# Sketch attention with a squared-ReLU MLP: first weights requested behind the first queries, values padded behind the key sketch copies, and a new planned order

## Chip, cores, metric

One core of one Trainium2 chip. The metric is the device time of one execution in microseconds (us), lower is better. The state of an execution ("fast" or "slow") is known from its time and from the granted TensorE clock in its records; only fast executions are compared unless the text says otherwise. Engines: PE (TensorE, matmuls), DVE (VectorE), ACT (ScalarE), POOL (GpSimd), SP (SyncE, which only issues DMAs here).

## What is computed

```python
# q, k, v: (4 batches, 4 heads, 1088 tokens, 32); S1, S2: (8, 32)
phi(x) = outer(S1 x, S2 x) flattened                 # 64 features per token
kv  = sum over tokens of phi(k) (x) v;  z = sum over tokens of phi(k)
attn = (phi(q) kv) / (phi(q) z + 1e-6)               # a sum over all tokens, not causal
x = attn transposed to (4352 tokens, 128)
out = relu(x @ w_in)**2 @ w_out                      # 128 -> 2048 -> 128
```

The MLP (called "expert" below) is most of the PE work. The attention of the next batch is fed in between its matmuls. Batches are numbered 0 to 3; "the third batch" is batch 2.

## The kernel before

The kernel lists some 620 small operations (`add`), each with the engines that may run it, an assumed duration, and a rank. A planner (`Graph.run`) simulates the engines with these durations and writes out one order; every engine then executes its part of this order strictly in turn. The ranks were found by a search outside of the kernel.

```python
def run(self):                                   # cut: the core of the planner
    ...
    t = max(eng_free.get(e, 0.0), t_slot)
    for d in o.deps: t = max(t, d.end + (SEM if d.eng != e else 0.0))
    ...
    if o.dma is not None:
        first = t + busy - 0.4 + DMA_FIRST       # + 0.4 on POOL
        pipe = max(pipe, first) + o.dma          # 1.85 us for a 544 KB load
        o.end = pipe + DMA_LAST + o.extra
```

Loads that convert or come late are requested by POOL. The first of them stands behind a `gate`, a one-column copy that reads data which must have landed, and each later group is chained: its request first reads one element (`gt`) of the load two groups earlier. The keys of the third and fourth batch also wait for `gate{b}`, a copy that reads the first normalised tokens of the batch before.

```python
o_gate = add("gate", {"POOL": (0.1, 0.15)}, lambda e: nc.gpsimd.tensor_copy(
    gate[96:128], vin[0][96:128, H - 1, 7, D - 1 : D]), [z_ops[0]], -45)   # first values
def cload(name, dst, src, probe, pri, dma, deps=(), new=True):
    ...
    def f(e):
        if mark: nc.gpsimd.tensor_copy(gt[:, 0:1], mark[1])      # waits for an earlier load
        nc.gpsimd.dma_start(out=dst, in_=src)
```

Per batch the attention does, among others (names as in the experiments):

```python
vp{b}.{a}   # ACT or POOL: values copied into a padded tile (a column of ones for z)
tk{b}.{p}   # DVE: keys transposed, kT <- kin, in two parts
ksk, ka, kp # PE sketch of the keys, ACT copy of it, product on DVE or POOL
tq{b}, qr   # DVE: queries transposed, qT <- qin; PE sketch of the queries
mx{b}.{g}   # DVE: den, rec, xs: normalisation of one group of output tokens
tx{b}.{g}, xe{b}.{g}   # PE transposition of xs, copy to xT: from here the expert can run
```

All PE start-up is covered by 30 filler matmuls on zeros (`warm0` to `warm29`, 128x512 each).

Of the kernel before, what the change touches and what calls it, by code (L numbers as in the profile page):

```python
# [19 lines left out]
DGE = 0.43  # L20


RANK = [
    165, 170, 191, 487, 140, 473, 83, 243, 387, 29, 569, 257, 275, 598, 621, 607, 623, 611, 618, 608, 596, 594,
    599, 602, 595, 610, 616, 617, 600, 605, 612, 614, 597, 609, 606, 603, 620, 619, 601, 613, 604, 622, 615,
    121, 85, 496, 286, 292, 31, 53, 582, 435, 476, 79, 120, 298, 526, 415, 475, 574, 355, 338, 160, 178, 10, 14,
    133, 365, 141, 57, 69, 104, 5, 2, 103, 126, 345, 26, 12, 306, 247, 314, 150, 9, 44, 152, 164, 71, 222, 4,
    74, 3, 55, 6, 100, 7, 93, 403, 182, 173, 507, 114, 539, 293, 76, 261, 80, 447, 384, 111, 215, 225, 366, 221,
    276, 299, 394, 17, 78, 92, 39, 145, 1, 135, 203, 193, 15, 98, 64, 52, 313, 382, 389, 357, 130, 369, 401,
    466, 212, 144, 579, 391, 370, 552, 456, 244, 518, 572, 327, 283, 498, 495, 530, 516, 262, 418, 591, 352,  # L30
    368, 564, 543, 485, 348, 477, 575, 316, 465, 302, 437, 542, 310, 188, 479, 201, 440, 49, 263, 147, 129, 199,
    67, 143, 11, 360, 367, 587, 511, 430, 450, 205, 541, 115, 59, 245, 464, 241, 482, 36, 171, 207, 444, 340,
    279, 537, 555, 218, 336, 86, 557, 109, 51, 554, 571, 66, 346, 406, 463, 264, 38, 489, 424, 124, 236, 25,
    250, 439, 371, 46, 350, 200, 392, 514, 154, 118, 8, 198, 18, 297, 206, 290, 524, 474, 462, 565, 592, 404,
    488, 139, 153, 142, 122, 374, 256, 134, 284, 27, 533, 81, 491, 535, 87, 556, 334, 443, 405, 106, 269, 326,
    268, 235, 540, 523, 503, 472, 460, 159, 578, 454, 397, 508, 558, 228, 41, 445, 509, 347, 23, 343, 300, 586,
    224, 291, 469, 471, 213, 28, 285, 20, 88, 50, 589, 77, 242, 33, 240, 132, 68, 398, 237, 204, 500, 90, 321,
    116, 515, 195, 289, 548, 303, 180, 184, 425, 412, 251, 234, 520, 429, 416, 156, 547, 329, 341, 317, 576,
    566, 560, 455, 502, 220, 380, 528, 480, 223, 181, 30, 32, 43, 75, 65, 166, 232, 22, 190, 499, 315, 97, 70,
    501, 72, 434, 127, 570, 417, 119, 158, 174, 373, 157, 253, 332, 484, 230, 214, 101, 532, 301, 238, 162, 216,  # L40
    231, 24, 378, 312, 172, 113, 358, 421, 82, 13, 359, 478, 529, 402, 255, 123, 442, 274, 61, 419, 559, 258,
    361, 45, 567, 536, 265, 525, 550, 545, 308, 395, 505, 583, 531, 325, 385, 590, 427, 335, 457, 110, 295, 519,
    561, 323, 544, 35, 73, 330, 62, 60, 233, 137, 91, 148, 63, 337, 48, 208, 95, 185, 146, 42, 458, 187, 112,
    167, 107, 163, 420, 58, 196, 287, 108, 149, 89, 362, 99, 331, 461, 383, 219, 410, 339, 483, 381, 273, 272,
    517, 259, 254, 436, 451, 534, 551, 319, 549, 584, 270, 356, 21, 453, 280, 490, 414, 553, 376, 521, 294, 396,
    581, 510, 513, 512, 282, 296, 426, 568, 131, 364, 438, 375, 94, 342, 136, 16, 278, 19, 209, 309, 486, 176,
    84, 56, 408, 177, 179, 493, 239, 105, 151, 311, 573, 40, 372, 432, 400, 47, 227, 192, 267, 102, 379, 328,
    585, 407, 377, 304, 506, 422, 563, 271, 189, 305, 527, 96, 428, 459, 186, 117, 217, 522, 37, 54, 388, 288,
    333, 210, 468, 399, 494, 229, 318, 183, 175, 249, 349, 413, 393, 277, 128, 562, 169, 252, 260, 497, 441,
    449, 588, 577, 593, 324, 246, 467, 452, 281, 322, 34, 492, 226, 307, 344, 125, 138, 353, 248, 538, 446, 433,  # L50
    155, 0, 431, 211, 390, 202, 351, 363, 386, 580, 546, 470, 409, 354, 481, 197, 423, 320, 411, 448, 266, 168,
    194, 504, 161,
# [3 lines left out]
    10: 1, 72: 1, 73: 0, 74: 1, 88: 1, 93: 1, 94: 0, 95: 1, 121: 1, 130: 0, 132: 0, 151: 0, 152: 1, 153: 0,  # L56
    174: 1, 178: 0, 187: 1, 188: 1, 202: 1, 207: 0, 208: 0, 209: 1, 210: 1, 234: 0, 242: 1, 244: 0, 258: 1,
    263: 1, 264: 1, 266: 0, 285: 0, 289: 1, 292: 1, 295: 0, 299: 1, 300: 1, 303: 0, 304: 0, 312: 1, 313: 0,
    316: 0, 317: 0, 320: 1, 324: 0, 328: 0, 329: 0, 332: 0, 333: 0, 336: 0, 337: 1, 341: 1, 349: 0, 350: 0,
    353: 0, 357: 0, 358: 0, 361: 0, 362: 1, 365: 0, 369: 0, 370: 0, 373: 1, 374: 0, 378: 1, 390: 0, 391: 1,  # L60
    395: 1, 398: 1, 399: 0, 403: 1, 406: 0, 407: 1, 410: 1, 411: 1, 414: 0, 415: 0, 418: 1, 419: 0, 427: 0,
    436: 1, 439: 0, 440: 0, 443: 0, 444: 0, 447: 0, 448: 0, 452: 0, 456: 1, 468: 0, 469: 0, 473: 1, 476: 0,
    480: 0, 481: 0, 484: 1, 485: 0, 488: 1, 492: 0, 496: 0, 505: 0, 506: 0, 509: 0, 510: 0, 513: 0, 518: 1,
    522: 1, 525: 0, 529: 0, 530: 0, 533: 1, 534: 0, 555: 1, 558: 0, 559: 0, 562: 0, 563: 0, 566: 0, 567: 1,
    571: 0, 574: 1, 584: 0, 587: 0, 592: 0, 595: 1, 604: 0, 608: 0, 609: 0, 613: 0, 616: 0, 617: 1,
# [10 lines left out]
class Op:  # L76
    def __init__(self, name, alts, fn, deps, pri, alloc, uses, port, dma, after, extra):
        self.extra = extra
        self.name, self.alts, self.fn, self.pri = name, alts, fn, pri
        self.deps = [d for d in deps if d is not None]  # L80
        self.alloc, self.uses, self.port, self.dma = alloc, uses, port, dma
        self.after = [d for d in after if d is not None]
        self.look = LOOK
        self.start = self.end = self.eng = None


class Graph:
# [22 lines left out]
    def run(self):  # L110
        eng_free, port_free, pipe, dge = {}, 0.0, 0.0, 0.0
        lanes = []
        todo = {id(o): len(o.deps) + len(o.after) for o in self.ops}
# [6 lines left out]
        while ready:  # L120
            cands = []
            for o in ready:
                t_slot = 0.0
# [12 lines left out]
                for e, (busy, lat, *pen) in o.alts.items():  # L136
                    pen = pen[0] if pen else 0.0
                    t = max(eng_free.get(e, 0.0), t_slot)
# [30 lines left out]
            eng_free[e] = t + busy  # L169
            if e in o.port:  # L170
                port_free = t + busy
# [32 lines left out]
def kernel(  # L204
# [11 lines left out]
    nc = tc.nc  # L216
# [63 lines left out]
    add = G.add  # L280
# [65 lines left out]
    o_gate = add("gate", {"POOL": (0.1, 0.15)}, lambda e: nc.gpsimd.tensor_copy(gate[96:128], vin[0][96:128, H - 1, 7, D - 1 : D]), [z_ops[0]], -45)  # L346
# [3 lines left out]
    def cload(name, dst, src, probe, pri, dma, deps=(), new=True):  # L350
# [10 lines left out]
        o = add(name, {"POOL": (0.85 if mark else 0.6, 3.0)}, f, gated + list(deps) + ([before[0]] if before else []), pri, dma=dma,  # L361
# [50 lines left out]
    def attention(b, vt):  # L412
# [16 lines left out]
        if b == 0:  # L429
            o_kh = [[add(f"ldk{b}.{c0}", SPQ, ld(kin[i], k, c0, c1), (), -230 + c0 / 8, dma=1.85 * (c1 - c0) / 34)] for c0, c1 in ((0, 16), (16, 34))]  # L430
            o_k, o_k2 = o_kh[0][0], o_kh[1][0]
            o_q = [add(f"ldq{b}.{c0}", SPQ, ld(qin[i], q, c0, c1), (), -227 + 2 * c0, dma=2.0 * (c1 - c0) / 34) for c0, c1 in QS]
# [13 lines left out]
            o_gate.deps += o_v[1]  # L446
# [57 lines left out]
        for part, (j0, j1) in enumerate(JP):  # L504
# [25 lines left out]
            prods.append(o_kp)  # L530
# [280 lines left out]
```

## Time and profile before

| | before |
|---|---|
| time, median of 3 runs | 120.3 us (119.84 to 120.82) |
| profiled execution: span, mean granted clock | 118.0 us, 0.995 |
| PE, DVE, ACT busy share | 92%, 82%, 78% |
| third batch's keys (544 KB): request, landing | 39.27, 43.81 (4.5 us later) |
| DVE's first transpose of these keys | starts at 44.07, no idle time ahead of it |

The lines that carry the argument are in the prediction. How to read the last two rows: an engine takes its instructions in the planned order, so a load only costs time when its reader reaches the head of its engine's queue before the load has landed. Here DVE has other work until the keys are in (it is busy with `g` until 44.15).

### The profile page before, as it was taken

To read this page: it belongs to the slowest core of one execution; us is meant where nothing else is said; L and a number is where in the kernel's file an instruction comes from. 1 tells how busy PE (TensorE), PEld (TensorE's weight loads), DVE (VectorE), ACT (ScalarE), POOL (GpSimd) and SP (SyncE) were. 2 spreads that over 40 slices of the span, in tenths; PEclk is the share of its full clock that TensorE was granted. 3 is DMA by queue.
4 is the path that set the end of the run, shared out by engine and by line. 5 is a ranking of instruction groups with operands and counts; after the bars stand their busy time and mean duration, and the time that the engine had idled before them with its cause. 6 is when DMAs were issued, how large, how long until landed. Compare 5 with 4: busy or idle time off the path is not lost.

```text
span 118.0 us, 3582 instructions
## 1 busy us (share of the span) xinstructions
PE 108.2 (92%) x1442; PEld 66.6 (56%) x1460; DVE 96.6 (82%) x179; ACT 91.9 (78%) x140; POOL 30.5 (26%) x73
## 2 busy tenths in 40 slices
PE   5998999999999998999999999999899999999850
PEld 2377676665666653555757545447656544567640
DVE  2658579989959699997559999999679989999920
ACT  0542367699885799999997999998649999999910
POOL 6139165593000764600006643300000000000000
PEclk9999999999999999999999999999999999999998
DMA  3960968774210299200401948102200050040522
GB/s 107 291 170 6 154 169 126 105 200 183 37 16 6 62 292 232 73 6 10 74 11 23 298 82 235 24 12 39 48 0 0 3 89 8 6 81 3 89 45 45
DMA packets 22272, 10.19 MB, mean 86 GB/s; under 512 B 19008, under 2 KB 20672, under 8 KB 22256
## 3 DMA queue, kind: packets, MB, share of 16 engines
q0 software_dynamic: 2688, 6.06, 20.6%
q1 hardware_dynamic: 18560, 3.54, 15.1%
q10 hardware_dynamic: 1008, 0.36, 1.4%
q8 instruction: 11, 0.18, 0.7%
q14 instruction: 5, 0.04, 0.1%
HBM read 8.78 MB, written 2.23 MB: 93 GB/s over the span
## 4 chain that ended last, share of the span: by engine, by line
PE 53%; ACT 18%; DVE 12%; issue 8%; DMA 4%; POOL 2%; DVEq 0%; ACTq 0%
PE o L724 16%; PE h L698 15%; ACT r L707 10%; PE h L629 6%; PE o L325 5%; DMA kin<-in_k_dram 4%; DVE g L717 4%; ACT g L715 3%; PE a L538 3%; PE h L583 2%; DVE qp L609 2%; PE a L496 2%; ACT A L598 2%; PE h L496 2%; DVE kT L476 1%
## 5 line engine op out<-in xcount | busy, mean ns | idle before, releaser
L707 ACT ACTIVATE r<-h 128x1024 bf16<-128x1024 f32 x53 | 52.0, 1046 | 4.6 <-PE h L698 3.3
L698 PE MATMUL h<-xT,w_in 128*128 128x512 bf16 (+1 forms) x152 | 36.2, 348 | 1.0 <-ACT r L707 0.7
L724 PE MATMUL o<-g,w_out 128*128 128x512 bf16 (+1 forms) x154 | 33.7, 346 | 1.5 <-DVE osb L731 0.5
L717 DVE TENSOR_TENSOR g<-r 128x1024 bf16<-128x1024 bf16 x46 | 30.6, 698 | 0.7 <-ACT r L707 0.3
L715 ACT ACTIVATE g<-r 128x1024 bf16<-128x1024 bf16 x22 | 23.7, 1089 | 0.2
L698 PEld LDWEIGHTS <-w_in 128*128 128x128 bf16 x160 | 16.6, 115 | 12.6 <-issue 3.1
L724 PEld LDWEIGHTS <-w_out 128*128 128x128 bf16 x160 | 15.1, 98 | 13.4 <-issue 1.6
L709 DVE TENSOR_SCALAR r<-h 128x1024 bf16<-128x1024 f32 x15 | 18.0, 1210 | 1.1 <-PE h L698 1.1
L609 DVE TENSOR_TENSOR qp<-h,A 128x512 f32<-128x512 f32 (+2 forms) x22 | 11.9, 562 | 2.9 <-ACT A L598 2.8
L598 ACT COPY A<-h 128x512 f32<-128x512 f32 (+2 forms) x22 | 10.0, 504 | 4.7 <-PE h L583 4.6
L629 PEld LDWEIGHTS h<-kvz,qp 128*64 128x64 f32 x288 | 9.2, 137 | 3.7 <-DVE qp L609 2.0
L583 PE MATMUL h<-qT,SR 32*64 32x256 f32 (+2 forms) x352 | 10.8, 338 | 0.1
L629 PE MATMUL h<-kvz,qp 128*64 128x66 f32 x288 | 10.4, 225 | 0.4 <-DVE kvz L553 0.2
L325 PE MATMUL o<-wz 128*128 128x512 bf16 x26 | 8.6, 450 | 1.5 <-DVE mk L288 1.2
L538 PEld LDWEIGHTS a<-vp,kp 128*64 128x64 f32 x216 | 6.9, 138 | 2.8 <-issue 2.2
L583 PEld LDWEIGHTS h<-qT,SR 32*64 32x64 f32 x352 | 6.2, 131 | 3.1 <-ACT r L707 0.8
L538 PE MATMUL a<-vp,kp 128*64 128x33 f32 x216 | 7.6, 224 | 0.2
L731 DVE STREAM_TRANSPOSE osb<-o 128x512 f32<-128x512 f32 (+1 forms) x10 | 6.3, 629 | 1.4 <-PE o L724 1.4
L663 POOL COPY gateb<-xs 128x1 bf16<-128x1 bf16 x3 | 0.6, 189 | 25.3 <-DVE xs L652 25.3
L360 POOL DMA_DIRECT2D vin<-in_v_dram x12 | 6.6, 560 | 0.4 <-issue 0.4
L476 DVE STREAM_TRANSPOSE kT<-kin 128x512 f32<-128x512 f32 x8 | 5.3, 681 | 1.4 <-DMA kin<-in_k_dram 1.4
L521 DVE TENSOR_TENSOR kp<-a,ka 128x512 f32<-128x512 f32 (+1 forms) x8 | 5.9, 747 | 0.5 <-ACT kb L511 0.5
(65 smaller groups left out, 88.5 us busy)
## 6 DMA issues: line engine op xcount, KB each, us to landing
kin<-in_k_dram POOLq DMA_DIRECT2D x3, 544.0 KB, 5.1
qin<-in_q_dram POOLq DMA_DIRECT2D x3, 544.0 KB, 3.6
vin<-in_v_dram POOLq DMA_DIRECT2D x12, 128.0 KB, 4.5
out_dram<-osb SPq DMA_DIRECT2D x16, 64.0 KB, 1.9
w_in<-in_moe_w_in_dram POOLq DMA_DIRECT2D x4, 128.0 KB, 3.7
w_out<-in_moe_w_out_dram POOLq DMA_DIRECT2D x4, 128.0 KB, 3.9
qin<-in_q_dram SPq DMA_DIRECT2D x1, 416.0 KB
out_dram<-osb SPq DMA_DIRECT2D x10, 32.0 KB, 1.6
```

The lines of the kernel that those rows point to most:

```text
L325: nc.tensor.matmul(tiles["o"][0][:, 0:512], wz[:, 0:128], wz, start=True, stop=True)
L538: nc.tensor.matmul(t[64 * (h % 2) : 64 * (h % 2) + 64, 33 * (h // 2) : 33 * (h // 2) + 33], kp[i][:, j, h, :], vp[i][:, h, j, :], start=(j ...
L583: nc.tensor.matmul(at(hb[x])[64 * y : 64 * y + 64, c0 : c0 + n], SR[32 * h : 32 * h + 32, ab].rearrange("p x y -> p (x y)"), rhs, start=Tr ...
L598: nc.scalar.copy(at(sA)[:, 0 : 2 * n].rearrange("p (r s) -> p r s", s=n), src(ab=0))
L609: nc.vector.tensor_tensor(out=o, in0=i0, in1=i1, op=ALU.mult)
L629: nc.tensor.matmul(at(nb)[64 * hf : 64 * hf + 64, col(x, pr)], qp[i][:, pr, n0 : n0 + 64], kvz[i][xx % 2][:, pr].rearrange("p y d -> p (y ...
L698: nc.tensor.matmul(at(hb)[:, step * w : step * w + N], w_in[:, 512 * (ct // E) : 512 * (ct // E) + 512].rearrange("p (c e) -> p e c", e=E) ...
L707: nc.scalar.activation(o, view(at(hb)), ACTF.Relu)
L709: nc.vector.tensor_scalar_max(o, view(at(hb)), 0.0)
L715: nc.scalar.activation(at(gb)[:, 0 : W * N], r, ACTF.Square)
L717: nc.vector.tensor_tensor(out=at(gb)[:, 0 : W * N], in0=r, in1=r, op=ALU.mult)
L724: nc.tensor.matmul(at(ob)[:, 0:N], w_out[:, ct, :], at(gb)[:, N * w : N * w + N], start=(ct == 0), stop=(ct == CT - 1))
```

## The change

Its intent: ask for the first weights earlier (behind the first queries, not behind the first values), pad batch 0's values only after its key sketch copies, correct some of the planner's durations by measured DMA latencies, charge a price for PE switching between wide and narrow work, and search the ranks again.

```diff
+SWITCH = 0.1
 RANK = [ ... ]   # all 624 ranks new (cut)
 SIDE = { ... }   # engine choices new (cut)
+def wide(o): return o.name[:2] in ("m1", "m2", "wa", "tx")
-                    t = max(eng_free.get(e, 0.0), t_slot)
+                    t = max(eng_free.get(e, 0.0) + (SWITCH if e == "PE" and wide(o) != last_wide else 0.0), t_slot)
-    o_gate = add("gate", ..., vin[0][96:128, H - 1, 7, D - 1 : D]), [z_ops[0]], -45)
+    o_gate = add("gate", ..., qin[0][96:128, 0:1]), pri=-45)
-        o = add(name, {"POOL": (0.85 if mark else 0.6, 3.0)}, ...
+        o = add(name, {"POOL": (1.15 if mark else 0.6, 3.0)}, ...
-            o_q = [add(f"ldq{b}.{c0}", ..., dma=2.0 * (c1 - c0) / 34) for c0, c1 in QS]
+            o_q = [add(f"ldq{b}.{c0}", ..., dma=2.0 * (c1 - c0) / 34, extra=0.0 if c0 else 1.5) for c0, c1 in QS]
-            o_gate.deps += o_v[1]
+            o_gate.deps.append(o_q[0])
+        if b == 0:
+            for o in o_vp: o.after.append(o_ka)
```

## The prediction

> **What bounds the kernel now.** I read the page first (busy shares, the 40 slices, the chain), then the chain in order of time, then a table of stretches, then the timeline from 4 to 26 us. All times in this text are microseconds of the profiled run (span 118.0) unless said otherwise.
>
> ```profile
> PE 108.2 (92%) x1442; PEld 66.6 (56%) x1460; DVE 96.6 (82%) x179; ACT 91.9 (78%) x140; POOL 30.5 (26%) x73
> PE   5998999999999998999999999999899999999850
> DVE  2658579989959699997559999999679989999920
> ACT  0542367699885799999997999998649999999910
> DMA  3960968774210299200401948102200050040522
> ```
>
> PE is nearly always busy, but part of that is filler: the page's group of warm-up matmuls (o<-wz) holds 8.6 us. Before about 24 us VectorE (DVE) and ScalarE (ACT) have holes; from there on all three are close to full. The DMA row has an empty slice, 8.85 to 11.8: the first loads are over and the next have not begun.
>
> ```profile
> 0.00:6.00 6.00, 4.78 (x16) 1.78 (x18) 2.84 (x14) 1.61 (x3) 2.54 (x15) 1.00 0.70 200
> 6.00:12.00 6.00, 5.40 (x143) 4.15 (x145) 4.17 (x8) 2.28 (x10) 3.98 (x8) 1.00 0.32 84
> 12.00:18.00 6.00, 5.75 (x139) 4.10 (x141) 3.97 (x11) 3.14 (x5) 2.44 (x8) 1.00 0.80 166
> 18.00:24.00 6.00, 5.64 (x81) 3.85 (x83) 5.84 (x13) 4.28 (x12) 3.43 (x9) 1.00 0.78 117
> 24.00:30.00 6.00, 5.93 (x65) 4.07 (x62) 5.70 (x7) 5.90 (x11) 3.68 (x7) 1.00 0.57 176
> 40.00:60.00 20.00, 19.00 (x264) 10.87 (x263) 16.79 (x30) 19.14 (x30) 6.37 (x13) 1.00 0.45 111
> 60.00:80.00 20.00, 19.48 (x227) 10.84 (x228) 18.82 (x34) 18.80 (x28) 7.00 (x14) 1.00 0.40 102
> 80.00:100.00 20.00, 19.62 (x245) 11.45 (x244) 17.90 (x32) 16.57 (x22) 0.00 (x0) 1.00 0.15 26
> ```
>
> Columns: stretch, length, busy time of PE, PEld, DVE, ACT, POOL, granted clock, DMA share, GB/s. The reader is to see two regimes: up to 24 us ACT is busy 11.3 of 24, after that no engine has more than a small reserve. So time can be won in two ways: by bringing work forward into the first 24 us, or by making PE and ACT lose less between pieces later.
>
> The chain shows what held the start:
>
> ```profile
> 10.21 0.18 POOL gate L346
> 10.39 0.71 POOL w_in L360
> 11.10 0.53 POOL w_out L360
> 11.63 5.07 DMA kin<-in_k_dram
> 16.72 0.71 DVE kT L476
> 17.43 0.13 DVE kT L478
> 17.56 0.59 DVE kT L476
> ```
>
> GpSimd (POOL) is in order. It reaches the gate only after padding values and a key product (kp, 9.08 to 10.15), then asks for the first weights and the second batch's keys. Those keys land at 16.70; the transpose that reads them stands in DVE's order ahead of batch 0's second output group and found DVE idle 0.76 us. The chain from there is work, not DMA. The timeline also shows the first values landing at 7.78 and the first queries' transpose starting at 5.77.
>
> **What the Trainium skill says.** "DMA: Bandwidth & Descriptors", section "SWDGE vs HWDGE vs iDMA": a casting DMA must come from GpSimd, and each DMA engine takes turns between the software and hardware queues. The weights cast to bf16, so they stay on POOL, and if asked for earlier they take turns with the values and queries still in flight from SP and ACT. Same page, "Issuing engines are not separate DMA queues": all issuers share the same 16 engines. The trace agrees as far as it goes: from 13 to 15 us, with only the software queue, the engines are 0.97 busy, so one queue alone fills them; the turns themselves have no case here. "TensorE: Matmul & The Clock Gate", section "Back-to-back issue gap", gives 518 cycles for 512 columns; here six such matmuls occupy 92.45 to 93.74, 215 ns each at granted clock 1.00, which agrees.
>
> **The change, part by part.**
>
> (1) The gate reads the first query piece instead of the first values, and in POOL's order it now stands ahead of the kp product, with no value padding before it. Queries land just before 5.77, so the gate fires near 5.8 instead of 10.21: 4.4 earlier. Issues of 0.77 + 0.55 + 0.55 follow, over near 7.7. Now the collision: issue to first movement was about 1.3 (10.34 to 11.7), so weights start moving near 7.2. The first loads ran at about 260 GB/s until 7.9 in the DMA view, so some 0.18 MB was left, 0.7 us of the engines. The keys were 5.07 behind their issue; moved by 4.4 and given back 0.7, they land near 16.70 - 4.4 + 0.7 = 13.0. The later weights chain on landings and move by the same 3.7: the second w_in was issued at 15.18 and would be at about 11.5. The bytes and the number of DMAs do not change.
>
> (2) Value padding of batch 0 goes from ACT and POOL in parallel to ACT alone, behind the key sketch copies. Both key sketch groups now run together on PE, so I estimate the copies (ka, kb) done near 8.0 instead of 8.77, then 0.62 + 0.62 + 0.61 of padding on ACT: done near 9.9. Before, padding ended at 9.00. The kv product needs the halves in turn (1.13 + 1.36 on PE from about 8.75), ending near 11.2 against 11.17. No gain, no loss.
>
> (3) New order. Instruction counts per engine stay almost the same: one relu of 128x1024 goes from DVE (1210 ns) to ACT (1046 ns), two xT copies from ACT to DVE, one kp from POOL (1.07) to DVE (0.64), one padding copy from POOL to ACT. This is rebalancing of about 1 us per engine.
>
> In the new DVE order the second batch's keys are transposed before and after the first output normalisation, all before the first xT copy. With a landing near 13.0 against a free DVE near 12.3, DVE would wait about 0.7, and the first xT comes near 15.6 instead of 14.57. That is the price. The return: 1.57 of transposes (0.71 + 0.20 + 0.66) and 0.66 of PE key sketch are done before the first expert matmul, which comes near 15.7 against 15.44. Following DVE's order with these durations, I get batch 0's last normalisation ending near 22.9 instead of 22.13, but with 1.6 more of kp done; ACT has done about 1.2 of value padding more by its last xT copy. That is 2.8 of elementwise work brought forward less the 0.8 slip: divided over two engines, 1.4 - 0.8 = 0.6, and with the first-layer matmuls no longer tied to late weights (one more 0.43 group done by then), about 1.0.
>
> (4) The planner now charges a price for PE switching between wide bf16 and narrow fp32 work. Counting neighbours in the two PE orders, the switches fall from 58 to 46, and from 38 to 28 after the first second-layer matmul. The trace shows a price: six wide ones after narrow work took 52.32 to 53.72, 1.40 against 1.29 without; two took 61.60 to 62.16, 0.56 against 0.43. So about 0.12 a round trip; ten fewer switches are five round trips, 0.6 of PE time. PE is 95 to 98% busy in that part, so I count it nearly whole, 0.5 to 0.6.
>
> (5) The number of warm-ups stays at 30, and 8 stand between first and last use of the filler after the first expert matmul in both. The filler is moved but not removed; no gain.
>
> Sum: -1.0 (start) - 0.6 (switches) and -0.3 for the rebalancing: ACT was 19.14 of 20 busy from 40 to 60, where any relief counts, but I cannot locate it. About -1.9 on 120.3: 118.4.
>
> **Rivals.** (a) The new DMA start collides: queries' rest and values are delayed, DVE stalls on its 128x832 query transpose (10.01 before) and kv waits for padding. For: the engines were 0.97 busy when one queue ran, and the first loads are not over at 7.2. Against: the values land by 7.78, mostly before the weights move. If the delay were 1.5 us, all of batch 0 shifts and the start gain is gone: about 119.5 to 120. (b) Earlier loads are hidden anyway: the chain after the keys is DVE and PE work, the only DMA wait removed is 0.76, and the order's quality decides. Then only switches count: 119.5. (c) The start gain carries whole: the weights 3.7 earlier fill the ACT holes up to 24 us, and the end moves by 2.5 to 3.5: 117. For: ACT has 12.7 idle in that time. Against: tokens, not weights, gate most of the first layer; the last xT of batch 0 lay at 23.9 and hardly moves in my count. (d) The final drain gets worse: the last stretch, 106 to 114, is a chain of relu, square, output matmul and transpose, and its new order is different; plus or minus 0.5.
>
> **Range and chances.** Rivals a and b pull to 119.5-120, c to 117. A planned order is seldom worse than the one it was searched against, and the run-to-run width of the old kernel is 119.84 to 120.82. I take 118.4, 8 in 10 between 116.7 and 120.2. Faster by 2% means below 117.9: 0.38. Slower by 2% means above 122.7: 0.04. Within: 0.58.
>
> **What would show it.** Gate near 5.8 and second-batch keys near 13.0; if they land after 14, the collision is larger than I think. DVE idle of about 0.7 at its first kT for batch 1. kv ending within 0.4 of 11.2. The first expert matmul at 15.2 to 16. ACT busier than 11.3 in the first 24 us, by 1 or more. PE idle and PE switching gaps in 30 to 100 lower by half a microsecond or more. The prediction is wrong if kv or the first expert matmul slips by over 1 us, or if ACT or DVE busy time after 24 us falls by clearly more than 1.5 us each.

## The result

The changed kernel is slower: 125.6 us median of 4 runs (124.16, 125.39, 125.82 in the fast state, 127.65 in the slow one), against 120.39 (119.84 to 120.82) for the kernel before on the same chip. The ratio is 1.0396, 95% interval 1.0292 to 1.05. Ratios here and below are the mean time of one kernel's fast runs over that of the other's of the same rounds, so not quite the ratio of the medians quoted. Not all "fast" executions are alike: of the three of the changed kernel only the 124.16 ran at a mean clock of 1.000, the other two at 0.985. The quickest alone is 3.2% over the mean of the kernel before (120.36), so some 0.8 of the 4.0% (an estimate) goes with the lower clock; section 1 comes back to it.

The profiled execution of the changed kernel is a fast one: 124.16 us, span 122.4, granted clock 1.0. First the stretches, in the columns that the prediction explained (stretch, length, busy time of PE, PEld, DVE, ACT, POOL, clock, DMA share, GB/s):

```profile
6.00:12.00 6.00, 5.98 (x129) 3.99 (x128) 4.09 (x8) 3.37 (x13) 3.10 (x5) 1.00 0.91 184
12.00:18.00 6.00, 5.40 (x120) 3.56 (x118) 4.66 (x14) 2.20 (x8) 3.76 (x10) 1.00 0.75 133
18.00:24.00 6.00, 5.76 (x124) 4.26 (x125) 4.79 (x11) 5.67 (x11) 3.76 (x9) 1.00 0.73 149
24.00:30.00 6.00, 4.94 (x76) 3.39 (x74) 4.28 (x7) 4.86 (x9) 0.61 (x1) 1.00 0.25 87
40.00:60.00 20.00, 17.42 (x217) 9.36 (x214) 16.35 (x29) 15.86 (x23) 5.60 (x11) 1.00 0.39 101
60.00:80.00 20.00, 19.61 (x228) 10.98 (x227) 17.57 (x32) 19.59 (x30) 5.05 (x12) 1.00 0.44 108
80.00:100.00 20.00, 19.88 (x302) 11.93 (x301) 16.43 (x30) 18.05 (x28) 1.26 (x1) 1.00 0.17 29
```

The early gap of the DMA engines is closed (share 0.91 in 6 to 12, 0.32 before), so that part of the intent worked. From 60 on PE is as busy as before or busier. Three stretches are worse: 12 to 18 (PE 5.40, before 5.75), 24 to 30 (4.94, before 5.93) and 40 to 60 (17.42, before 19.00). The last is one hole. The same four microseconds of both kernels, before first:

```profile
44.00:48.00 4.00, 3.57 (x45) 1.84 (x43) 4.00 (x7) 4.00 (x8) 2.30 (x6) 1.00 0.96 234
```

```profile
44.00:48.00 4.00, 1.77 (x10) 0.65 (x8) 2.05 (x7) 2.81 (x4) 1.33 (x4) 1.00 0.21 41
```

The chain of waits of the changed kernel, in order of time, names what ended the hole (start, duration, what):

```profile
21.35 4.04 DMA vin<-in_v_dram
...
39.24 6.62 DMA kin<-in_k_dram
...
45.92 0.60 issue
```

Of the old chain DMA was 4%, of this one 22%. The timeline of DVE and PE in the changed kernel shows who waited (start, duration, engine, line, operation, in brackets the idle time ahead of it and what ended it):

```profile
41.49 1.28 DVE L728 TENSOR_TENSOR g<-r 128x1024 bf16<-128x1024 bf16 x2
45.88 0.71 DVE L484 STREAM_TRANSPOSE kT<-kin 128x512 f32<-128x512 f32 x1 [3.11 <-DMA kin<-in_k_dram]
46.52 0.13 DVE L658 TENSOR_SCALAR den<-h 128x16 f32<-128x16 f32 x1
...
47.07 0.69 DVE L663 TENSOR_TENSOR xs<-h,rec 128x512 bf16<-128x512 f32 x1
```

```profile
47.82 0.61 PE L682 MATMUL a<-ident,xs 128*128 128x128 bf16 x5 [2.23 <-DVE xs L663]
```

And the same work of DVE in the kernel before:

```profile
40.66 0.17 DVE L647 TENSOR_SCALAR den<-h 128x16 f32<-128x16 f32 x1 [1.10 <-PE h L629]
...
41.24 0.69 DVE L652 TENSOR_TENSOR xs<-h,rec 128x512 bf16<-128x512 f32 x1
...
44.07 1.29 DVE L476 STREAM_TRANSPOSE kT<-kin 128x512 f32<-128x512 f32 x2
```

The reader is to see the swap. Before, DVE normalises the second batch's last output group (den to xs) first and transposes the third batch's keys three microseconds later. In the changed order the first transpose of those keys stands *ahead* of the normalisation. DVE is idle for 3.11 us, with the transpose at the head of its queue. The matmuls that the normalisation needs end at 43.33, so for the last 2.5 us the work behind it was ready; `xs` comes late, the PE transposition that needs `xs` comes late, and the expert's next tokens with it.

Two facts meet there. The planner thought the keys would be in: its own table has the request at 34.64, landing at 39.29, the transpose at 39.41 and the normalisation at 40.01. And the landing itself was slow: 6.6 us from the request, against 4.5 in the kernel before with a request at the same time (39.24 and 39.27).

Where did the time go in all? I took, for each PE transposition (the moments where new tokens reach the expert), its start time less the attention and expert work of PE that stands ahead of it in program order (fillers left out), with the same durations for both kernels, and compared that lag:

| lag of the changed kernel against before, us | 1st transposition | 3rd | 4th (38.1) | 5th (47.8) | end |
|---|---|---|---|---|---|
| changed kernel | 1.63 | 1.31 | 2.26 | 4.66 | 4.4 |

So 2.3 us are lost by 38 us, 2.4 more at the hole, and a quarter of a microsecond is won after it. Kernels that ran within 0.5% of the kernel before show lags of 0.3 to 1.3 at the end by this measure, in part because the profiled execution of before was a quick one (119.76 us); end lags under that mean little.

The early loss has two visible parts. A set-up matmul with the sketch weights (`SX`) stands behind 12 fillers instead of 9. It started at 6.44 us, 4.76 before (a kernel with the same PE order, `a_early2` below, had it at 5.32, so much of the difference is the run's own). And at 26 us PE waited 1.06 us for a PSUM bank, because ACT did two value paddings of the second batch ahead of batch 0's last xT copy.

### The profile page after: what moved, and what is told of

Read it like the earlier page. It is cut to its first block, busy times and chain, and to the rows that moved or that the text cites. A ratio compares the mean times of both kernels' runs of the same rounds, so it can differ in the third digit from the quotient of the medians.

```text
span 122.4 us, 3597 instructions
## 1 busy us (share of the span) xinstructions
PE 111.3 (91%) x1460; PEld 66.9 (55%) x1460; DVE 95.4 (78%) x178; ACT 95.1 (78%) x147; POOL 27.6 (23%) x67
## 3 DMA queue, kind: packets, MB, share of 16 engines
HBM read 8.78 MB, written 2.23 MB: 90 GB/s over the span
## 4 chain that ended last, share of the span: by engine, by line
PE 44%; DMA 22%; issue 15%; ACT 7%; POOL 4%; DVE 3%; SPq 1%; POOLq 0%
PE h L709 17%; PE o L735 15%; DMA kin<-in_k_dram 9%; DMA qin<-in_q_dram 4%; ACT r L718 4%; PE a L549 4%; DMA w_out<-in_moe_w_out_dram 4%; DMA vin<-in_v_dram 3%; PE h L594 3%; PE h L640 3%; ACT g L726 2%; POOL vin L368 1%; DMA out_dram<-osb 1%; DVE osb L742 1%; PE a L504 1%
## 5 line engine op out<-in xcount | busy, mean ns | idle before, releaser
L718 ACT ACTIVATE r<-h 128x1024 bf16<-128x1024 f32 x54 | 52.8, 1030 | 3.4 <-PE h L709 3.1
L709 PE MATMUL h<-xT,w_in 128*128 128x512 bf16 (+1 forms) x160 | 37.0, 350 | 0.4 <-ACT xT L688 0.3
L735 PE MATMUL o<-g,w_out 128*128 128x512 bf16 (+1 forms) x160 | 35.8, 347 | 1.0 <-DVE osb L742 0.9
L720 DVE TENSOR_SCALAR r<-h 128x1024 bf16<-128x1024 f32 x14 | 17.0, 1214 | 0.8 <-PE h L709 0.8
L333 PE MATMUL o<-wz 128*128 128x512 bf16 x30 | 10.7, 482 | 1.2 <-DVE mk L296 1.2
L594 PE MATMUL h<-qT,SR 32*64 32x256 f32 (+2 forms) x352 | 11.4, 339 | 0.0
L549 PEld LDWEIGHTS a<-vp,kp 128*64 128x64 f32 x288 | 9.0, 138 | 3.8 <-issue 2.0
L549 PE MATMUL a<-vp,kp 128*64 128x33 f32 x288 | 9.9, 224 | 1.1 <-ACT xT L688 1.1
L529 POOL TENSOR_TENSOR kp<-kb,ka 128x512 f32<-128x512 f32 x3 | 3.4, 1131 | 14.2 <-PE o L735 9.7
```

The source lines that it names most:

```text
L333: nc.tensor.matmul(tiles["o"][0][:, 0:512], wz[:, 0:128], wz, start=True, stop=True)
L549: nc.tensor.matmul(t[64 * (h % 2) : 64 * (h % 2) + 64, 33 * (h // 2) : 33 * (h // 2) + 33], kp[i][:, j, h, :], vp[i][:, h, j, :], start=(j ...
L594: nc.tensor.matmul(at(hb[x])[64 * y : 64 * y + 64, c0 : c0 + n], SR[32 * h : 32 * h + 32, ab].rearrange("p x y -> p (x y)"), rhs, start=Tr ...
L709: nc.tensor.matmul(at(hb)[:, step * w : step * w + N], w_in[:, 512 * (ct // E) : 512 * (ct // E) + 512].rearrange("p (c e) -> p e c", e=E) ...
L718: nc.scalar.activation(o, view(at(hb)), ACTF.Relu)
L720: nc.vector.tensor_scalar_max(o, view(at(hb)), 0.0)
```

## The experiments

All edits act on the planned order, just before it is written out, through one helper:

```diff
     order = G.run()
+    def shift(name, anchor, behind=0):     # move one operation to just ahead of (or behind) another
+        o = next(x for x in order if x.name == name)
+        order.remove(o)
+        order.insert(next(i for i, x in enumerate(order) if x.name == anchor) + behind, o)
```

Theory 1: the early place of the third batch's key transpose on DVE costs most of the 4%. Rival: the late start does, and the hole only absorbs slack.

### 1. One mend each, both, and the same fault put into the kernel before

`a_head` mends the start of the changed kernel, `a_k2` moves the one transpose back, `a_head_k2` does both, `b_k2early` puts the transpose early in the kernel *before*.

```diff
 # a_head                                    # a_k2
+shift("ST", "tk0.1")                       +shift("tk2.0", "tk2.1")
+shift("SX", "warm9")                        # a_head_k2: both
+for n in (13, 12):                          # b_k2early, in the kernel before
+    shift(f"warm{n}", "ksk0.3", 1)         +shift("tk2.0", "mx1.1")
```

> The changed kernel with one stretch of its order put back as it was: on PE the small setup matmul stands behind nine warm-ups instead of twelve, two more warm-ups go behind the key sketch, and on DVE the transpose that feeds the setup matmul stands ahead of the second key transpose again. Theory A (the start lost 1.6 us because the setup matmul queued behind cold warm-ups, and it is carried to the end): first expert matmul near 15.6 instead of 17.14, and 1.2 to 1.8 us off the changed kernel's time, some 123.7. Rival (the later wait for the third batch's keys sets the end anyway): under 0.5 us off, 124.8 or more.

> The changed kernel with one instruction moved on DVE: the first transpose of the third batch's keys stands behind the second batch's last normalisation, next to the second such transpose, not ahead of it. Theory B (DVE, in order, stood 3.1 us at that transpose waiting for the keys' landing, and PE 2.2 us behind it): 2.0 to 2.8 us off, some 122.8, and no DVE wait on the keys near 43 to 46. Rival (the loss is general, from PE order and balance, and the wait is only where it shows): under 0.7 us off.

> Both moves together. Theories A and B together: the two losses lie one after the other, so 3.4 to 4.4 us off, 121 to 121.8, within 1 us of the kernel before. Rival (they overlap): no more than the larger of the two alone, 122.8.

> The kernel before with the one move the other way round: its first transpose of the third batch's keys stands ahead of the second batch's last normalisation. Theory B: the keys were issued at 39.3 and landed at 43.9 in the kernel before while its normalisation began at 40.7, so DVE would stand some 3 us and the time rise by 2 to 3, to 122.5 to 123.5. Rival (this kernel's slack absorbs it): under 0.7 us more.

| | median, us (range) | ratio to before [95%] |
|---|---|---|
| a_head | 123.03 (122.43 to 124.16) | 1.0212 [1.0115, 1.0309] |
| a_k2 | 125.42 (122.94 and 124.71 fast, 126.12 and 127.11 slow) | 1.0267 [1.0111, 1.0423] |
| a_head_k2 | 125.91 (125.67 to 126.55) | 1.0447 [1.0365, 1.053] |
| b_k2early | 123.95 (123.41 to 124.9) | 1.0303 [1.0193, 1.0414] |

`b_k2early` is the clean one: a single DVE operation moved, 3% lost, and the profile has the same hole:

```profile
44.38 0.71 DVE L476 STREAM_TRANSPOSE kT<-kin 128x512 f32<-128x512 f32 x1 [3.95 <-DMA kin<-in_k_dram]
45.01 0.13 DVE L647 TENSOR_SCALAR den<-h 128x16 f32<-128x16 f32 x1
```

But `a_k2` did not mend the changed kernel (its two fast runs average 1.3 points better, inside the intervals), and both mends together were worse than one. The timeline of `a_k2` shows what is left (its profiled execution is a slow one; the rows lie ahead of its clock dip, which begins at 54.2):

```profile
47.47 1.29 DVE L484 STREAM_TRANSPOSE kT<-kin 128x512 f32<-128x512 f32 x2
48.68 0.21 DVE L486 STREAM_TRANSPOSE kT<-kin 128x64 f32<-128x64 f32 x1
51.17 0.71 DVE L573 STREAM_TRANSPOSE qT<-qin 128x512 f32<-128x512 f32 x1 [2.28 <-DMA qin<-in_q_dram]
```

The lag at the fifth transposition fell from 4.66 to 2.56, as theory 1 has it, but the third batch's queries were next. Their request is chained to the landing of the keys (46.05 there, request at 47.02, landing at 51.14). The wait moved down the chain of requests. So the order exposes a *chain* of late loads, and moving one reader only changes which of them is met.

In the profiled executions of `a_k2` and `a_head_k2` the granted clock fell as well, to a half, for 3.4 and 6.8 us. The stretches of `a_head_k2`, whose profiled run counts as fast:

```profile
48.00:52.00 4.00, 1.76 (x25) 1.04 (x24) 1.65 (x5) 4.00 (x8) 0.75 (x2) 1.00 0.70 165
52.00:56.00 4.00, 3.40 (x36) 1.75 (x35) 4.00 (x6) 1.60 (x4) 0.82 (x1) 0.51 0.02 4
56.00:60.00 4.00, 3.67 (x15) 1.46 (x12) 1.52 (x4) 1.50 (x4) 0.00 (x0) 0.63 0.00 0
```

PE is idle for 2.24 us of the first line, in two waits of 0.92 and 1.21 us, and the clock (third column from the end) is at a half from 52.1 to 58.9. The Trainium skill, "TensorE: Matmul & The Clock Gate", section "HAM oscillation — how this bites in real kernels", describes this answer to a PE that waits for DMA, and gives gaps over about 3.4 us as its condition. The half clock agrees; the gaps here were shorter. Their length alone does not decide it: PE waited 2.23 us in the changed kernel and 2.55 in `b_k2early` with no such dip in the profile, and 2.21 in `a_pad` (section 3) with one of 3.4 us. A half clock for 6.8 us costs up to 3.4 us (an estimate from these two numbers), which is the size of the difference between fast and slow executions of one kernel below: the slow profiled executions of `a_head_early2` and `a_early2_pad` have one dip of 6.8 us each, which begins near 28 us, 1.5 and 1.9 us behind the end of a PE wait of 2.1 and 1.2 us. So a hole can cost more than its length, and may be part of why the mends above do not add up; no run separates the two.

### 2. The request earlier instead of the reader later; and each part of the change alone

`a_early2` moves the requests of the third batch's keys, values and queries up POOL's order, right behind the second batch's value padding (25.67 us for the keys instead of 39.24). `a_head_early2` adds the start mend. `b_headlate` and `b_gate` put one part of the change each into the kernel before: the late set-up matmul, and the early first weights.

```diff
 # a_early2
+last = "vp1.1"
+for n in ("ldk2", "ldv2.0", "ldv2.1", "ldv2.2", "ldv2.3", "ldw2", "ldq2"):
+    shift(n, last, 1); last = n
 # b_headlate, in the kernel before             # b_gate, in the kernel before
+shift("ST", "tk0.1", 1)                       -gate reads vin[0][96:128, H - 1, 7, D - 1 : D]
+for n in (9, 10, 11):                         +gate reads qin[0][96:128, 0:1]
+    shift(f"warm{n}", "SX")                   +for n in ("gate", "w_in0", "w_out0", "ldk1"):
                                               +    shift(n, "vp0.1")
```

> The changed kernel with the third batch's keys, values and queries requested some 14 us earlier: right after the second batch's queries and its first value padding on GpSimd, without the gate that waits for the second batch's normalisation. Their buffers have long been read by then. No engine's compute order changes. Theory B (the loss near 40 to 48 is DVE standing in order before keys that land 6.6 us after their request): no wait of DVE on keys or queries of the third batch, PE busy over 19 of 20 from 40 to 60, and 2.0 to 3.0 us off the changed kernel, some 122.5. Rival (the order is bad there whatever lands, as the run with the moved transpose, which got slower again later, might suggest): under 0.7 us off.

> The same early requests, with the start mended too as in the run that put the setup matmul behind nine warm-ups. Theories A and B together: that run's 123.0 less 2.0 to 3.0, so 120 to 121, level with the kernel before. Rival: 122.3 or more.

> The kernel before with the start of the changed kernel's order: the small setup matmul stands behind twelve warm-ups on PE, and the transpose that feeds it behind the second key transpose on DVE. Theory A: the first twelve warm-ups take 0.43 us each, so the setup matmul starts near 6.4 instead of 4.76, and batch 0 and the end come 0.9 to 1.7 us later, 121.4 to 122.2. Rival (the keys of the second batch, whose landing at 16.7 stands in the chain, hide it): under 0.5 us.

> The kernel before with the earlier gate alone: the gate reads the first queries, and it and the first weights' and second keys' requests stand ahead of the value padding on GpSimd; the order of PE, DVE and ACT is the old one. My prediction's part 1 (requests 4.4 us earlier, keys near 13, no DVE wait of 0.76 on them): 0.3 to 1.0 us faster than before, 119.5 to 120.1. Rival (the weights share the DMA engines with the values, padding and kv come later): as before or up to 1 us slower.

| | median, us (range) | ratio [95%] |
|---|---|---|
| a_early2 | 121.33 (121.08 to 121.44 fast, one slow 124.55) | 1.007 [1.0019, 1.0121] |
| a_head_early2 | 121.41 (121.15 to 121.58 fast, one slow 124.9) | 1.007 [1.0019, 1.012] |
| b_headlate | 120.56 (120.54 to 121.89) | 1.004 [0.9975, 1.0106] |
| b_gate | 120.21 (120.06 to 120.42) | 0.9985 [0.9942, 1.0028] |

With the same DVE order, but the loads asked for in time, 4.0% became 0.7%. In `a_early2` the first transpose still stands ahead of the normalisation, and follows its predecessor without a wait:

```profile
40.86 1.28 DVE L728 TENSOR_TENSOR g<-r 128x1024 bf16<-128x1024 bf16 x2
42.06 0.70 DVE L484 STREAM_TRANSPOSE kT<-kin 128x512 f32<-128x512 f32 x1
42.81 0.18 DVE L658 TENSOR_SCALAR den<-h 128x16 f32<-128x16 f32 x1
```

The start mend, worth 1.8% alone, is worth nothing on top. Theory 1 holds, with one addition: what costs is the early place together with a load that is not yet in. Its rival is limited to what the hole did not already cover. The late set-up matmul alone is not distinguishable from nothing (0.4%). Nor are the earlier weights alone (-0.15%): the lag does fall by a microsecond between the first and second transposition of the changed kernel (1.63 to 0.59), as the prediction reckoned (the key sketch of the second batch stands there in place of six fillers), and is spent again by the fourth.

### 3. The ACT order, all mends, and controls

`a_pad` moves batch 0's last xT copy ahead of two value paddings of the second batch on ACT; the next two combine it with the mends above; `b_early2` gives the early requests to the kernel before.

```diff
 # a_pad
+for n in ("vp1.2", "vp1.0"):
+    shift(n, "xe0.2", 1)
 # a_early2_pad, a_head_early2_pad: with the shifts above;  b_early2: the shifts of a_early2, in the kernel before
```

> The changed kernel with one move on ACT: the copy of batch 0's last transposed tokens out of PSUM stands ahead of the second batch's value padding, not behind it. In the changed kernel's trace the padding waited 1.1 us for a late landing, the copy behind it with it, and PE 1.1 us for the PSUM bank that the copy frees. Theory C (a third wait in order, before a transfer): 0.7 to 1.3 us off the changed kernel if the later stall stays as it is, some 124.2. Rival (the stall on the third batch's keys swallows it, since those are requested when the second batch's normalisation ends): no, they would move with it; less than 0.4 us off would mean that PE's wait there is covered by something else.

> The same move on top of the early requests for the third batch. Theories B and C: 121.3 less 0.7 to 1.3, so 120.0 to 120.6, and no more executions of 124 or above[...]. Rival: 121 or more, with some executions still near 124.5.

> All three mends on the changed kernel: start, early requests, padding. If the changed order is otherwise as good as my prediction thought (0.6 us from fewer PE switches and about 1 us from the earlier weights), it ends at 118.5 to 119.5, faster than both. If only the waits were at fault and the rest of the order is merely as good as the old one, 120 to 120.6.

> Control: the kernel before with the same early requests for the third batch. Its order stands behind those loads with slack (DVE began the key transpose just after the landing, with work done meanwhile), so theory B says no change, within 0.4 us. Were it over 1 us faster, the early requests would be a gain of their own and the changed kernel's recovery no sign of its order.

| | median, us | ratio [95%] |
|---|---|---|
| a_pad | 123.23 (one of four slow) | 1.0193 [1.0144, 1.0242] |
| a_early2_pad | 121.31 (one of four slow, 124.25) | 1.0046 [1.0005, 1.0087] |
| a_head_early2_pad, 5 rounds | 120.89 (120.73 to 121.17, six of six fast) | 1.0028 [1.0002, 1.0055] |
| b_early2 | 120.56 (120.27 to 120.64) | 0.9995 [0.9963, 1.0027] |

The control `b_early2` shows that early requests are worth nothing where DVE does not wait: their gain in the changed order is the hole and not some general benefit. With all three mends the changed order is back within 0.3% of the kernel before, and no execution was slow; its profile has no PE wait over 0.7 us. The expectation for `a_early2_pad` (no more executions of 124 or above) missed: one of four took 124.25, with PE still waiting 1.2 us at 25. So three places of the new order account for nearly all of the loss; nothing beyond the old time is left over as a gain.

### 4. Is the landing slow because POOL asks? And one more try at a faster version

The keys took 6.0 to 6.6 us from request to landing in every kernel of the changed order with the late request so far, and 4.2 to 4.5 in the old order. `a_k2sp` lets SP's hardware queue ask for them, behind the first output's stores. `a_all_split` takes all mends and splits the padding of batch 0 between POOL and ACT again.

```diff
 # a_k2sp
-            nc.gpsimd.dma_start(out=dst, in_=src)
+            (nc.sync if name == "ldk2" else nc.gpsimd).dma_start(out=dst, in_=src)
+shift("ldk2", "st0.3", 1)
 # a_all_split: the shifts of a_head_early2_pad, and
+next(x for x in order if x.name == "vp0.1").eng = "POOL"; shift("vp0.1", "ldk1", 1)
+shift("vp0.2", "ka0.3", 1); shift("vp0.0", "ka0.3", 1)
+for n, a in ((14, "kv0.3"), (15, "kv0.3"), (16, "qr0.1"), (17, "qr0.1")): shift(f"warm{n}", a, 1)
```

> The changed kernel with one request moved: the third batch's keys are asked for by the sync engine's queue, at about the same time (behind three of the first output's four stores, near 38.5), not by GpSimd. The compute order is the changed one. If the 6.0 to 6.6 us landing lies with GpSimd's descriptors: landing 3.5 to 4.5 us after the request, DVE's wait 3.1 down to 1 or less, 1.8 to 3 us off the changed kernel's time. Rival (the transfer itself is slow at that time, whoever asks): landing over 6 us, under 0.7 us off.

> All three mends, and the start's values padded half on GpSimd as in the kernel before, with four warm-ups moved from ahead of the kv product to behind it and behind the second query product. If part 2 of the change cost what the mended kernel still lacks: first transposes 0.3 to 0.6 us earlier than in the three-mend run and 120.3 to 120.6, level with the kernel before. Rival (the rest lies in the order from 24 us on): 120.8 to 121.0 as before.

`a_k2sp`: 125.03 us (two of four slow), ratio 1.0277 [1.0178, 1.0376]; the keys were asked for at 38.0 and took 7.2 us (the profile is of a slow execution, but its clock dip begins at 48.7, after the landing). It is the transfer that is slow, whoever asks. `a_all_split`: 120.76 (120.5 to 121.88), ratio 1.0019 [0.9967, 1.007]: no different from `a_head_early2_pad` and no better than the kernel before.

### 5. Why the landing is slow: the stores

A first suspect was the first output's four stores (small packets of 128 bytes), which run in the changed order just ahead of the keys. `a_latestore` issues them behind those of the second output.

```diff
+for n in ("st0.0", "st0.1", "st0.2", "st0.3"):
+    shift(n, "st1.3", 1)
```

> The changed kernel with the four stores of the first output group issued behind those of the second, and nothing else moved. It asks why the third batch's keys took 6.6 us to land in the changed kernel against 4.5 before. Theory (the many small packets of those four stores, issued in the 3 us around the request, hold the keys up): the stores then start after 47 us, the keys land in 4.7 or less from their request, DVE waits 1.2 or less at their first transpose instead of 3.11, and the ratio to the kernel before falls from 1.04 to 1.015 to 1.03. Rival (the landing is slow for a reason other than the stores): 5.8 to 6.8 from request to landing again, DVE waits 2.3 to 3.3, ratio 1.03 to 1.045.

124.95 us (123.65 to 125.46 fast, one slow 125.69), ratio 1.0261 [1.0176, 1.0346]. No store left before 50.85, and the keys took 6.9 us; DVE waited 3.3. The stores are ruled out.

What the slow landings look like is in the DMA view from 38 to 48 us, 40 slices of 0.25 us, DMA share in tenths and GB/s. Before, then changed:

```profile
DMA  0000000000786899899999999696979987999897
GB/s 0 0 0 0 0 0 0 0 0 0 191 244 226 244 348 435 328 401 383 296 213 229 213 197 221 114 186 137 186 114 164 280 216 271 411 411 302 334 250 147
```

```profile
DMA  1616073000945799989689899954000000010000
GB/s 18 115 16 116 15 119 77 0 0 0 157 70 191 313 435 383 398 336 347 182 247 329 198 247 189 164 90 66 8 16 16 33 16 16 8 33 0 0 0 0
...
q8 instruction: 1, 0.02, 0.8%
```

Both reach the same rates with the keys and the values behind them (up to 435 GB/s). In the changed kernel a tail of 8 to 33 GB/s then drags on from 45.0 to 47, far less than the engines together can do. The trace's list of packets shows where it starts: eight of the keys' 128 rows, the share of one of sixteen engines, run one after another from 41.68 (the first takes 1.13 us), and the last starts 4.9 us behind the request (3.5 before). That one engine is behind with its share fits this; the trace does not name the engines. The changed kernel's view also has one packet of the instruction queue q8, which the view before lacks. The Trainium skill, "Runtime: NRT & Kernel Launch", section "Instruction fetch mechanics", says that an engine's instructions come in blocks of 16 KiB, 256 instructions, through a DMA queue of its own. The trace agrees: both kernels have 11 such packets in queue q8, and between the first and the last of them PE runs 121 matmuls, each with its weight load, per packet on average (about 242 instructions). So I take it that the packet's time follows from how many PE instructions went before; `a_fetch` below tests this. Over all kernels so far with the late request:

| kernel | instruction packet starts, us after the keys' request | keys land after, us |
|---|---|---|
| before, b_k2early, b_headlate, b_gate | -2.1, -2.1, -2.3, -2.2 | 4.5, 4.2, 4.3, 4.3 |
| changed, a_head, a_head_k2, a_pad | 0.4, 0.2, 0.5, 0.4 | 6.6, 6.0, 6.5, 6.6 |
| a_k2, a_latestore, a_k2sp | 0.7, 0.3, 1.7 | 6.5, 6.9, 7.2 |

### 6. Why the landing is slow: the instruction packet moved

Theory 2: the packet (0.9 to 1.7 us long) is what delays one engine's share. For it: in the changed kernel, `a_head`, `a_pad`, `a_latestore` and `a_k2` the row that takes long (1.13 us in the changed kernel) starts 0.8 to 1.0 us after the packet has ended. Rival: a coincidence. `a_fetch` cuts the first 14 fillers of the changed kernel into four each, 84 more PE instructions of the same total width. `b_fetch` and `b_fetch2` try the reverse in the kernel before, to bring the next packet behind the request.

```diff
 # a_fetch
-  nc.tensor.matmul(o[:, 0:512], wz[:, 0:128], wz, start=True, stop=True)
+  w = 128 if n < 14 else 512
+  for c in range(0, 512, w):
+      nc.tensor.matmul(o[:, c : c + w], wz[:, 0:128], wz[:, c : c + w], start=True, stop=True)
 # b_fetch: w = 64 if n < 3 else 128, weight wz[:, 0:32], output o[0:32];  b_fetch2: 32 instead of 64
```

> The changed kernel with each of the first 14 warm-up matmuls cut into four of 128 columns, so that PE runs 84 more instructions (42 matmuls, 42 weight loads) before its first expert work and nothing else differs. In all seven profiled kernels of the changed order with the late request, one 16 KB packet of the instruction queue fell between 0.0 and 0.8 us after the request of the third batch's keys or within the time the transfer ran, and the keys took 6.0 to 7.2; in the four of the old order it fell 2.1 to 2.3 us before the request, and they took 4.2 to 4.5. [...]the 84 more move that packet from 39.6 to about 36.5. Theory (the instruction packet holds one of the 16 DMA engines, and that engine's share of the keys lands last): the packet starts 2 or more before the request, the keys land in 4.9 or less, the first transpose waits 1.5 or less instead of 3.11, and the ratio falls from 1.04 to 1.015 to 1.03. Rival (the packet is a coincidence): the packet moves, the landing stays at 5.8 or more, ratio 1.03 to 1.045.

> The reverse, in the kernel before: the 30 warm-ups cut into smaller ones (the first three into eight, the rest into four, with a weight of 32 columns), 204 more PE instructions, so that the next instruction packet, at 51.8 so far, falls near 39.8, half a microsecond behind the request of the third batch's keys at 39.3. Theory: they land in 5.8 to 6.8 instead of 4.5, with the old order's DVE not waiting for it more than 1 us longer; the time is the same within 1.5% (the order leaves room). Rival: 4.2 to 4.8 as before although the packet is there. If the packet misses the stretch from 0 to 1 us after the request the run does not decide.

> As b_fetch (the kernel before with its warm-ups cut smaller), with the first three warm-ups cut into sixteen instead of eight: 48 more PE instructions, to move the instruction packet from 0.95 us behind the request of the third batch's keys to about 0.2 to 0.6 behind it, where it lay in the slow landings of the changed order. Theory A (a packet that starts within the 0.56 us in which GpSimd writes the request delays the keys, one that starts later does not): landing 5.8 or more. Rival B (the packet is not what delays them, and the cut warm-ups cured the changed kernel in another way): 4.2 to 4.8. If the packet falls outside 0 to 0.75 us after the request, neither is decided. The time is read for nothing here.

| | median, us | ratio [95%] | packet after request | landing | DVE idle ahead of the transpose |
|---|---|---|---|---|---|
| a_fetch | 121.19 (121.0 to 121.67) | 1.0049 [0.9982, 1.0117] | -3.4 | 4.3 | 0.82 |
| b_fetch | 122.35 (122.03 to 122.8) | 1.0144 [1.0062, 1.0226] | +0.96 | 4.6 | none |
| b_fetch2, one run | 121.52 (before: 119.83) | not timed | -2.2 | 4.3 | none |

`a_fetch` keeps the changed order on DVE, ACT and POOL and the late request. Nothing was done but to cut fillers, and the loss fell from 4.0% to 0.5%, within noise of none. The first transpose still stands ahead of the normalisation, and waits 0.82 us:

```profile
42.66 0.71 DVE L486 STREAM_TRANSPOSE kT<-kin 128x512 f32<-128x512 f32 x1 [0.82 <-DMA kin<-in_k_dram]
43.30 0.14 DVE L660 TENSOR_SCALAR den<-h 128x16 f32<-128x16 f32 x1
```

Its start was also 0.8 us earlier than in the profile of the changed kernel, but so was that of `a_head`, with the same lag of 0.86 at the first transposition; `a_head` had a landing of 6.0 and stayed at 1.0212. The difference between these two is the landing.

The reverse did not succeed. In `b_fetch` the packet fell 0.96 us behind the request, at the very edge of the stretch that I had named, while the transfer was about to begin, and the keys still came in 4.6. In `b_fetch2` it fell 2.2 us ahead, so that run decides nothing. By the letter `b_fetch` speaks for the rival: the mere presence of a packet behind the request is not enough. The fourth batch's keys, asked for at 62 to 68 us, say the same in the runs on record: in six kernels (the one before, `b_k2early`, `b_headlate`, `b_gate`, `b_early2`, `b_fetch2`) a packet fell 0.7 to 1.1 us behind that request, and the landing took 4.3 to 5.7 us, median 5.0; in the other fourteen, without one there, 4.2 to 5.1, median 4.4. That is half a microsecond, not two. What is shown is that the landing was slow in all seven kernels with the packet 0.2 to 1.7 us behind, and that 84 extra PE instructions, which moved the packet 4.7 us earlier, cured it. That the packet itself is the cause, and if so why not in `b_fetch`, stays open. The time of `b_fetch` itself is not read for this: its fillers and its start changed with it.

No version beats the kernel before: `b_gate` at 0.9985 is within noise of it.

## Why the prediction was wrong

**The bound and the opening.** Right. PE stayed near full wherever its feed held. The second batch's keys landed at 13.3 (predicted 13.0), but with luck: the gate fired at 6.8 (predicted 5.8) and the keys were asked for at 8.6 (7.2 by my count), and the 0.7 us that I gave the collision did not appear; they took 4.7 us, not 5.8.

**Part 1, start, -1.0.** The microsecond is there between the first and second transposition (lag 1.63 to 0.59, where the work takes the place of six fillers), but starting from a loss that I had not counted (the set-up matmul behind 12 fillers), and it is not carried on: `b_gate` alone gives 0.15%. Rival (b), earlier loads hidden anyway, was right on this point.

**Part 2, padding, no gain and no loss.** Not separable: `a_all_split`, which undoes it, differs by less than its interval. I wrote that kv would end within 0.4 of 11.2; it ended near 12.8, because of the late set-up matmul and the fillers and the query product placed ahead of it. The first expert matmul came at 17.14 (predicted near 15.7, before 15.44). Both are over the 1 us that I had named as a sign of being wrong.

**Part 3, new order, included in the start and -0.3 for the rebalancing.** This is the step that failed. I followed the new DVE order against the old only through the first 24 us, where I did find the keys of the *second* batch pulled ahead of a normalisation and priced it at 0.7 (it cost nothing: DVE came to them at 13.91, after the landing, late itself). The same swap for the third batch, at 40 us, stood in the same list, and I did not price it. The runs put 3.1 us of DVE idle time and 2.2 of PE there. In its place I had the sentence "A planned order is seldom worse than the one it was searched against", which is no argument: the planner had the landing at 39.29 and it came at 45.86. The term that I left out has two factors, the place of the reader and the latency of the load: with the landing at 4.3 us the same place cost 0.82 us of DVE idle time and 0.5% (`a_fetch`); in the old order, whose DVE gets there sooner, it cost 3.95 us and 3.0% even at 4.2 (`b_k2early`). I also misread the rebalancing: not one but three large and two small padding copies went from POOL to ACT, 2.5 us, and ACT's busy time rose from 91.9 to 95.1 us.

**Part 4, fewer PE switches, -0.5 to -0.6.** Not seen. Between the fifth transposition and the end the lag falls from 4.66 to 4.4, and from 1.37 to 1.1 in `a_head_early2_pad`: 0.26 to 0.27 in both, under half of what I counted, and within what this measure can tell from noise.

**Part 5, fillers: moved, no gain.** Wrong in sign: three of them ahead of the set-up matmul were part of the late start, though alone this is at most 0.4% (`b_headlate`).

**The rivals.** None had a new in-order wait in the middle of the kernel. Rival (a) put a collision of DMAs at the start. I also took a load's latency from the old kernel as a constant; it was 4.5 there and 6.6 in the new one, and why is not settled. And no rival had the clock fall behind a hole.

**The chance of slower by 2%, 0.04,** came from that same sentence, and was far too low for a change that replaces all ranks.

## What to carry to other kernels

When an order is replaced, list for every load its request, its landing and the place of its first reader on the in-order engine, for the whole kernel and both orders; a reader that has moved ahead of ready work is a cost as large as the landing is late. Mend it at the request, not at the reader, when requests are chained: moving one reader met the next late load, moving the requests up removed 3.3 of 4.0%. And treat a DMA latency as a range: the same 544 KB took between 3.9 and 7.2 us here, so a plan that needs it within a few tenths is fragile.

## What the Trainium skill lacked or had wrong

- "DMA: Bandwidth & Descriptors", section "Anatomy of one DMA — SWDGE (gpsimd) path": its fit, 2.0 us plus bytes over 436e3 per us, gives an estimate of 3.3 us for the 544 KB load of keys. For the third batch's keys the runs have 3.9 to 6.9 from POOL and 7.2 from SP's queue, with the values' requests right behind, so here the fit was a lower bound.
- "Runtime: NRT & Kernel Launch", section "Instruction fetch mechanics", calls the cost of a new instruction block mostly hidden. Its 16 KiB packets are visible here, 0.9 to 1.9 us each on the DMA engines, and seven kernels in which PE's packet fell 0.2 to 1.7 us behind a load's request had that load 2 us late. 84 more PE instructions moved the packet and cured it (6.6 to 4.3 us); one kernel with the packet 0.96 us behind was not slow (4.6), and the fourth batch's keys lost about 0.6 us (median 5.0 against 4.4), so the cause is not settled.
- "TensorE: Matmul & The Clock Gate", section "HAM oscillation — how this bites in real kernels", names idle gaps over about 3.4 us. In `a_head_k2` two waits of 0.92 and 1.21 us within three microseconds were followed by a half clock for 6.8 us, while single waits of 2.23 us (the changed kernel) and 2.55 (`b_k2early`) were not.
- No page that I read says that such a clock loss in the middle of a kernel sets some of its executions apart: `a_early2` ran at 121.1 to 121.4 us and once at 124.55, with a mean clock of 0.99 to 1.00 and of 0.965.
